# Delta rule over one chunk of all 32 heads at a time, in 64x64 tiles on the quadrants of the array

## The chip, the cores and the metric

One core of a Trainium2 chip runs the program. The metric is the device time of one execution in microseconds (us). Times of parts come from one execution that the hardware profiler took. The engines are named PE (TensorE, matmuls), PEld (TensorE's weight loads, which overlap PE), DVE (VectorE), ACT (ScalarE), POOL (GpSimd) and SP (SyncE, which issues most DMAs).

## What is computed

The first stage is a delta rule over 4 batches x 8 heads, 768 tokens, head size 48, all float32. The second sends each token to one of 8 experts by the largest logit, and an expert keeps at most 80 tokens, those with the largest gate weight.

```python
k_n = k / (np.linalg.norm(k, axis=-1, keepdims=True) + 1e-06)
state = np.zeros((B, H, D, D))
for t in range(S):
    y[:, :, t] = einsum('bhd,bhde->bhe', q[:, :, t], state)
    v_old = einsum('bhde,bhd->bhe', state, k_n[:, :, t])
    state = state + beta[:, :, t, None, None] * einsum('bhd,bhe->bhde', k_n[:, :, t], v[:, :, t] - v_old)
x = y.transpose(0, 2, 1, 3).reshape(B * S, H * D)          # 3072 x 384
# mixture of experts: 8 experts, hidden size 1024, capacity 80
logits = x @ w_gate; expert_idx = argmax(logits); gate_w = softmax(logits)[expert_idx]
for e in range(8):
    tok_idx = the at most 80 tokens of expert e with the largest gate_w
    out[tok_idx] = gate_w[tok_idx, None] * (np.maximum(x[tok_idx] @ w1[e], 0) @ w2[e])
```

## The kernel before

The delta rule runs in chunks of C = 64 tokens. Within a chunk, with A[t, s] = beta_s k_t.k_s for s < t, it is Z = (I + A)^-1 (V - K S), U = beta Z, y = Q S + (Q K^T, s < t) U, S += K^T U. The inverse is built from blocks of width 1, 2, 4 to 64: five levels after the first, each with a product P2 of B1 (which holds I + A transposed) and X, masked, then a new X and its transpose Y.

A tile holds two heads: 128 rows are (head of the pair, token of the chunk), and the matrices that multiply them are block-diagonal over the two heads, 128x128 with two zero blocks. A step is one chunk of one batch: four pairs of heads side by side, 128x512 in one PSUM bank. There are 48 steps, handled two at a time.

`prep(i)` (L229 to L289) makes what a step needs without the state: the scaled k and a copy of q go into block-diagonal tiles `kbd` and `qbd` on POOL (L234, L236), four transposes each give KT and QT (L241, copied by ACT at L242), K K^T and Q K^T are products (L246, L248) whose evictions on DVE apply beta and the mask (L251, L252), two selects and a product on POOL make B1 and the first Y (L253 to L258), and a transpose of B1 gives the first X (L262, L264). Each of the five levels has a product (L269) evicted by DVE with a mask (L271), a product (L276) copied by ACT to X (L278) and the transpose of X (L283) copied by ACT to Y (L287); the last level makes Y alone, by a product (L285).

`chain(i)` (L294 to L350) is the part that needs the state: K S (L303), R = V - K S on DVE (L305), Z and U (L309, L311), y (L317, L318) copied by ACT (L331) and written by two DMAs to `x_rows` in DRAM (L334), the new state (L322, L328; kept in SBUF, added on DVE), and the gate's logits by a transpose and small products (L338 to L349, 64 weight columns, 8 moving).

`weave` (L421) takes one stage of each of its generators in turn, so the order of every engine's queue is: one stage of the chains of two steps, one stage of each of the next two preps, and so on. In the loop at L439 each pass handles two steps of one batch. PSUM holds five one-bank buffers for prep (`ps_m`) and three for the chain (`ps_c`). `norms(b)` (L190) gives the inverse norms of k for a whole batch; `load(b)` (L153) loads k, q and v of a batch on the SP queue. `gate(b)` (L352) turns a batch's logits into weights and keeps the 80 best candidates by ten rounds of maxima and replacements (L408, L409) on DVE.

After the last step, the candidates are gathered by six DMAs into `mg` (L484), the threshold is found on DVE (L489, L491), slots are computed, and tokens are gathered and sent through the experts (L568 on). Expert matrices are 16 tiles of 1.57 MB loaded by `load_w` on the SP queue: WR0 = 4 of them during the delta rule, six (WR - WR0) when its memory is free (L460), the others as experts finish.

In the profile a float32 product is two matmul instructions with a weight load each; a transpose is one of each.

Of the kernel before, what the change touches and what calls it, by code (L numbers as in the profile page):

```python
# [24 lines left out]
def kernel(  # L25
# [26 lines left out]
    NP = H // 2  # L52
# [5 lines left out]
    NM = B * NT  # L58
# [4 lines left out]
    PD = NP * D  # L63
    GP = 2 * D
    assert NP == 4 and GP <= 128 and NT * E <= 128 and 2 * E * NM <= 512

# [9 lines left out]
    strict = const.tile([128, 128], F32, name="strict")  # L76
    nc.gpsimd.memset(strict, 1.0)
    nc.gpsimd.affine_select(out=strict, in_=strict, compare_op=Alu.is_gt, fill=0.0, base=0,
                            pattern=[[1, 128]], channel_multiplier=-1)
# [7 lines left out]
    for w in widths:  # L87
        m = const.tile([128, 128], F32, name=f"mask{w}")
        nb = 128 // (2 * w)
        mv = m.rearrange("p (g j) -> p g j", g=nb)  # L90
        nc.gpsimd.memset(mv[:, :, w:], 0.0)
        lo = mv[:, :, 0:w]
        nc.gpsimd.memset(lo, -1.0)
        nc.gpsimd.affine_select(out=lo, in_=lo, compare_op=Alu.is_ge, fill=0.0, base=-w,
                                pattern=[[-2 * w, nb], [0, w]], channel_multiplier=1)
        nc.gpsimd.affine_select(out=lo, in_=lo, compare_op=Alu.is_ge, fill=0.0, base=2 * w - 1,
                                pattern=[[2 * w, nb], [0, w]], channel_multiplier=-1)
        nc.gpsimd.affine_select(out=m, in_=m, compare_op=Alu.not_equal, fill=1.0, base=0,
                                pattern=[[1, 128]], channel_multiplier=-1)
        masks.append(m)  # L100
    mask1T = const.tile([128, 128], F32, name="mask1T")
    nc.gpsimd.memset(mask1T, 0.0)
    odd = mask1T.rearrange("p (g j) -> p g j", j=2)[:, :, 1:2]
    nc.gpsimd.memset(odd, -1.0)
    nc.gpsimd.affine_select(out=odd, in_=odd, compare_op=Alu.is_equal, fill=0.0, base=0,
                            pattern=[[-2, 64], [0, 1]], channel_multiplier=1)
    nc.gpsimd.affine_select(out=mask1T, in_=mask1T, compare_op=Alu.not_equal, fill=1.0, base=0,
                            pattern=[[1, 128]], channel_multiplier=-1)
# [5 lines left out]
    hii = const.tile([128, NM], I32, name="hii")  # L114
    nc.gpsimd.iota(hii, pattern=[[2, NM]], base=0, channel_multiplier=0)
    hi = const.tile([128, NM], F32, name="hi")
    nc.gpsimd.tensor_copy(hi, hii)
    pp1i = const.tile([128, 1], I32, name="pp1i")
    nc.gpsimd.iota(pp1i, pattern=[[1, 1]], base=1, channel_multiplier=1)
    pp1 = const.tile([128, 1], F32, name="pp1")  # L120
    nc.gpsimd.tensor_copy(pp1, pp1i)

    beta_t = keep.tile([128, B, NP, NC], F32, name="beta_t")
    wg = keep.tile([GP, NP // 2, 2, E], F32, name="wg")
# [6 lines left out]
    WR0, WR = 4, 10  # L131
# [10 lines left out]
    with ExitStack() as actx:  # L142
        inp = actx.enter_context(tc.tile_pool(name="inp", bufs=2))
        blk = actx.enter_context(tc.tile_pool(name="blk", bufs=1))
        mat = actx.enter_context(tc.tile_pool(name="mat", bufs=4))
        vec = actx.enter_context(tc.tile_pool(name="vec", bufs=3))
# [4 lines left out]
        kin, qin, vin, inv, state = {}, {}, {}, {}, {}  # L151

        def load(b):  # L153
            if b >= B:
                return
            for lst, nm, src in ((kin, "kin", k), (qin, "qin", q), (vin, "vin", v)):
                t = inp.tile([128, NP, NC, D], F32, name=nm)
                for h in range(H):
                    p, e = divmod(h, 2)
                    nc.sync.dma_start(t[64 * e : 64 * e + 64, p],  # L160
                                      src[b, h].rearrange("(c t) d -> t c d", t=C))
                lst[b] = t

        half = B // 2 * NP * NC
        bt = blk.tile([half, 2, 2, C], F32, name="bt")
        for j in range(2):
            for e in range(2):
                for r in range(half // NC):
                    b, p = divmod(r + j * (half // NC), NP)
                    nc.scalar.dma_start(bt[r * NC : (r + 1) * NC, j, e, :],  # L170
                                        beta[b, 2 * p + e].rearrange("(c t) -> c t", t=C))
        load(0)
        for h in range(H):
            p, e = divmod(h, 2)
            g, p2 = divmod(p, 2)
# [14 lines left out]
        def norms(b):  # L190
            if b >= B:
                return
# [426 lines left out]
```

## Time and profile before

| | |
|---|---|
| runs, median (lowest to highest) | 1162.03 us (1161.6 to 1165.42) |
| span of the profiled execution | 1162.0 us |
| instructions | 21302, of them 8825 matmuls and as many weight loads |
| PE busy | 1056.7 us |
| DVE, ACT, POOL busy | 439.1, 326.7, 236.3 us |

A span counts from the first to the last instruction of the program. Busy times of PE and PEld overlap, and matmuls are pipelined: the recorded duration of one (some 280 ns) is longer than the distance to the next, so a pace is read from a run of equal instructions in the timeline.

### The profile page before, as it was taken

To read this page: it belongs to the slowest core of one execution; us is meant where nothing else is said; L and a number is where in the kernel's file an instruction comes from. 1 tells how busy PE (TensorE), PEld (TensorE's weight loads), DVE (VectorE), ACT (ScalarE), POOL (GpSimd) and SP (SyncE) were. 2 spreads that over 40 slices of the span, in tenths; PEclk is the share of its full clock that TensorE was granted. 3 is DMA by queue.
4 is the path that set the end of the run, shared out by engine and by line. 5 is a ranking of instruction groups with operands and counts; after the bars stand their busy time and mean duration, and the time that the engine had idled before them with its cause. 6 is when DMAs were issued, how large, how long until landed. Compare 5 with 4: busy or idle time off the path is not lost. (4 is left out here: it accounts for less than half of the span.)

```text
span 1162.0 us, 21302 instructions
## 1 busy us (share of the span) xinstructions
PE 1056.7 (91%) x8825; PEld 993.7 (86%) x8825; DVE 439.1 (38%) x982; ACT 326.7 (28%) x609; POOL 236.3 (20%) x436
## 2 busy tenths in 40 slices
PE   0799999999999999999999999999999999704998
PEld 0789999999999999999999999998999999704775
DVE  3352333433433624534335333344345323364010
ACT  1234223423322343333234223333332342100000
POOL 3320222032212202221220223023112201002000
PEclk9999999999999999999999999999999999755999
DMA  7930401400200005002000000000000000361820
GB/s 119 211 140 18 155 7 23 71 8 11 43 5 7 6 5 89 5 5 48 8 5 5 8 5 7 6 8 5 5 8 8 5 5 8 93 241 34 275 72 13
DMA packets 116863, 52.22 MB, mean 45 GB/s; under 512 B 103456, under 2 KB 111648, under 8 KB 116768
## 3 DMA queue, kind: packets, MB, share of 16 engines
q1 hardware_dynamic: 114720, 48.79, 17.8%
q0 software_dynamic: 768, 1.97, 0.6%
q8 instruction: 70, 1.15, 0.4%
q10 hardware_dynamic: 1280, 0.11, 0.1%
q14 instruction: 25, 0.20, 0.1%
HBM read 40.42 MB, written 10.42 MB: 44 GB/s over the span
## 5 line engine op out<-in xcount | busy, mean ns | idle before, releaser
L269 PE MATMUL pm<-X,B 128*128 128x128 f32 x1920 | 244.1, 281 | 3.6 <-DVE X L264 3.4
L269 PEld LDWEIGHTS pm<-X,B 128*128 128x128 f32 x1920 | 228.2, 195 | 8.9 <-DVE X L264 8.4
L271 DVE TENSOR_TENSOR P<-pm,mask 128x512 f32<-128x512 f32 x240 | 165.5, 690 | 172.7 <-PE pm L269 168.7
L278 ACT COPY X<-pm 128x512 f32<-128x512 f32 x192 | 112.4, 585 | 363.5 <-PE pm L276 363.4
L276 PE MATMUL pm<-P,Y 128*128 128x128 f32 x1536 | 195.4, 280 | 1.0 <-DVE ohg L388 0.5
L276 PEld LDWEIGHTS pm<-P,Y 128*128 128x128 f32 x1536 | 179.5, 191 | 9.3 <-issue 2.6
L287 ACT COPY Y<-pm 128x512 f32<-128x512 f32 x240 | 138.4, 588 | 104.7 <-PE pm L285 63.3
L283 PE MATMUL pm<-ident,X 128*128 128x128 f32 x768 | 117.4, 281 | 5.2 <-ACT X L278 3.5
L236 POOL COPY qbd<-qin 64x192 f32<-64x192 f32 x96 | 32.7, 342 | 387.8 <-PE pm L241 382.9
L283 PEld LDWEIGHTS pm<-ident,X 128*128 128x128 f32 x768 | 85.0, 145 | 16.2 <-ACT X L278 14.8
L234 POOL TENSOR_TENSOR kbd<-kin,inv 64x192 f32<-64x192 f32 x96 | 48.9, 509 | 220.3 <-PE pc L322 199.4
L318 PE MATMUL pc<-U,PT 128*128 128x48 f32 x384 | 73.0, 277 | 0.3 <-DVE U L311 0.2
L331 ACT COPY xs<-pc 128x192 f32<-128x192 f32 x48 | 15.3, 318 | 188.6 <-PE pc L318 188.3
L317 PE MATMUL pc<-st,QT 128*128 128x48 f32 x352 | 66.2, 270 | 0.0
L258 POOL TENSOR_TENSOR Y<-B,mask1T 128x512 f32<-128x512 f32 x48 | 60.9, 1269 | 4.0
L311 DVE TENSOR_TENSOR U<-pc,beta_t 128x192 f32<-128x192 f32 x48 | 17.2, 358 | 111.2 <-PE pc L309 111.2
L318 PEld LDWEIGHTS pc<-U,PT 128*128 128x128 f32 x384 | 58.3, 195 | 0.5 <-DVE U L311 0.5
L317 PEld LDWEIGHTS pc<-st,QT 128*128 128x128 f32 x352 | 54.4, 195 | 0.0
L246 PE MATMUL pm<-KT 128*128 128x128 f32 x384 | 53.1, 282 | 0.0
L248 PE MATMUL pm<-QT,KT 128*128 128x128 f32 x384 | 51.6, 278 | 0.0
L579 PEld LDWEIGHTS hp<-xTe,w 128*128 128x128 f32 x384 | 49.0, 210 | 2.1 <-issue 1.2
L285 PE MATMUL pm<-Y,P 128*128 128x128 f32 x384 | 49.0, 280 | 0.5
(153 smaller groups left out, 1232.8 us busy)
## 6 DMA issues: line engine op xcount, KB each, us to landing
w<-in_moe_w_dram SPq DMA_DIRECT2D x16, 1536.0 KB
kin<-in_k_dram SPq DMA_DIRECT2D x32, 144.0 KB
qin<-in_q_dram SPq DMA_DIRECT2D x32, 144.0 KB
vin<-in_v_dram SPq DMA_DIRECT2D x32, 144.0 KB
x_rows<-xs SPq DMA_DIRECT2D x96, 48.0 KB
out_dram<-zero SPq DMA_DIRECT2D x12, 384.0 KB
bt<-in_beta_dram ACTq DMA_DIRECT2D x32, 3.0 KB
wg<-in_moe_w_gate_dram ACTq DMA_DIRECT2D x8, 1.5 KB
```

Source lines behind the costliest of these rows:

```text
L246: nc.tensor.matmul(pk[:, p, :], lhsT=KT[:, p, :], rhs=KT[:, p, :], start=True, stop=True)
L248: nc.tensor.matmul(pq[:, p, :], lhsT=KT[:, p, :], rhs=QT[:, p, :], start=True, stop=True)
L258: nc.gpsimd.tensor_tensor(out=Y, in0=B1, in1=over_pairs(mask1T), op=Alu.mult)
L269: nc.tensor.matmul(pp[:, p, :], lhsT=B1[:, p, :], rhs=X[:, p, :], start=True, stop=True)
L271: nc.vector.tensor_tensor(out=P2, in0=pp, in1=over_pairs(masks[n]), op=Alu.mult)
L276: nc.tensor.matmul(px[:, p, :], lhsT=Y[:, p, :], rhs=P2[:, p, :], start=True, stop=True)
L278: nc.scalar.copy(X, px)
L283: nc.tensor.transpose(py[:, p, :], X[:, p, :], ident)
L285: nc.tensor.matmul(py[:, p, :], lhsT=P2[:, p, :], rhs=Y[:, p, :], start=True, stop=True)
L287: nc.scalar.copy(Y, py)
L317: nc.tensor.matmul(py[:, p, :], lhsT=QT[:, p, :], rhs=state[b][:, p, :], start=True, stop=False)
L318: nc.tensor.matmul(py[:, p, :], lhsT=PT[:, p, :], rhs=U[:, p, :], start=(c == 0), stop=True)
```

## The change

The work is cut the other way: a block is one chunk of all 32 heads, and there are 12 blocks. Heads are named by (g, p, e): row half e (partitions 0 to 63 or 64 to 127), bank p, and one of NQ = 8 places g. A matrix of one head is 64x64 on one half of the partitions, with no zero blocks, and 32 of them fill a tile of 128 x 2 x 8 x 64 (two PSUM banks). Every product except the transposes of K, Q and x and the logits is done per head, with 64 (or 48) contracted rows and up to 64 output rows, so it uses one quadrant of the array: the row half of its operands and the column half of its output. `tiles` emits the 32 products so that consecutive ones go to the quadrants (0, 0), (1, 1), (0, 1), (1, 0) in turn, and the table `lv` says in which half and bank each level's results stand, so that tiles of different row halves write different banks.

- `prep(c)`: K and Q are transposed from unpadded pairs of heads (16 transposes per block, 128x128). B1 is turned into X by a product with `eye` instead of a transpose; Y is made at each level as a product of P2 and the old Y, not as a transpose of X. Evictions are two halves of 128 x 512 each. The copy of q on POOL is gone (q is loaded into `qn` directly); the selects on B1 are done per half of the partitions, over 1024 columns.
- `chain(c)`: Q S and the masked Q K^T U are evicted separately and added on DVE. The state is accumulated by PE in PSUM (`S_ps`, two banks) and copied to SBUF by ACT. x of a block is 128 rows (two batches) x 2 x 384.
- PSUM: `ps_m` has three buffers of two banks, used by prep, chain and gate alike; `S_ps` has the other two banks.
- Loads are per chunk (`load_k`, `load_q`, `load_v`), norms too. `w_gate` is loaded by one DMA. WR0 is 2 instead of 4.
- Loop: pass c weaves `chain(c)`, the second half of `prep(c + 1)` (7 stages) and the first half of `prep(c + 2)` (7 stages). The gate runs once every three blocks.

```diff
-    WR0, WR = 4, 10
+    WR0, WR = 2, 10
...
-        mat = actx.enter_context(tc.tile_pool(name="mat", bufs=4))
+        mat = actx.enter_context(tc.tile_pool(name="mat", bufs=3))
-        ps_m = actx.enter_context(tc.tile_pool(name="ps_m", bufs=5, space=PSUM))
-        ps_c = actx.enter_context(tc.tile_pool(name="ps_c", bufs=3, space=PSUM))
+        ps_m = actx.enter_context(tc.tile_pool(name="ps_m", bufs=3, space=PSUM))
+        ps_s = actx.enter_context(tc.tile_pool(name="ps_s", bufs=1, space=PSUM))
...
+        def mtile():
+            return ps_m.tile([128, 2, 512], F32, name="pm", tag="m")
...
+        def tiles(where, emit, byhead=False):
+
+            cls = {}
+            for e, p, g in HEADS:
+                cls.setdefault(where(e, p, g) if byhead else where(e, p), []).append((e, p, g))
+            order = [kk for kk in ((0, 0), (1, 1), (0, 1), (1, 0)) if kk in cls]
+            for n in range(max(len(x) for x in cls.values())):
+                for kk in order:
+                    if n < len(cls[kk]):
+                        emit(*cls[kk][n])
...
+        def halves(fn):
+            for n in range(2):
+                fn(slice(4 * n, 4 * n + 4))
...
+            KT = mat.tile([128, NQ, 128], F32, name="KT")
+            QT = mat.tile([128, NQ, 128], F32, name="QT")
+            for dst, src in ((KT, kb), (QT, qb)):
+                pt = mtile()
+                for g in range(NQ):
+                    nc.tensor.transpose(pt[:, g // 4, (g % 4) * 128 : (g % 4) * 128 + 128],
+                                        src[:, 2 * g : 2 * g + 2, :].rearrange("r p d -> r (p d)"), ident)
+                for n in range(2):
+                    nc.scalar.copy(dst[:, 4 * n : 4 * n + 4], pt[:, n].rearrange("r (g w) -> r g w", w=128))
+            yield
+            pk, pq = mtile(), mtile()
+            for ps, r in ((pk, KT), (pq, QT)):
+                tiles(lambda e, p: (p, e),
+                      lambda e, p, g: nc.tensor.matmul(ps[hs(e), p, 64 * g : 64 * g + 64],
+                                                       lhsT=KT[hs(p, D), g, hs(e)], rhs=r[hs(p, D), g, hs(e)],
+                                                       start=True, stop=True))
...
+            px = mtile()
+            tiles(lambda e, p: (e, e),
+                  lambda e, p, g: nc.tensor.matmul(px[hs(e), p, 64 * g : 64 * g + 64],
+                                                   lhsT=B1[hs(e), p, g], rhs=eye[hs(e)], start=True, stop=True))
+            X = mat.tile([128, 2, NQ, 64], F32, name="X", bufs=2)
...
+            lv = {1: (EE, PP, PP, PP, EE), 2: (PP, EE, PP, EP, PP), 3: (EP, EE, EP, PP, EP), 4: (PP, EE, PP, EP, PP),
+                  5: (EP, EE, None, EP, PP)}
+            xb, yb = PP, PP
+            for n in range(1, len(widths)):
+                f, pb, xo, yh, yo = lv[n]
+                last = n == len(widths) - 1
+                pp = mtile()
+                tiles(lambda e, p: (e, f(e, p)),
+                      lambda e, p, g: nc.tensor.matmul(pp[hs(f(e, p)), pb(e, p), 64 * g : 64 * g + 64],
+                                                       lhsT=B1[hs(e), p, g], rhs=X[hs(e), xb(e, p), g],
+                                                       start=True, stop=True))
+                P2 = mat.tile([128, 2, NQ, 64], F32, name="P2", bufs=2)
+                halves(lambda s: nc.vector.tensor_tensor(out=P2[:, :, s], in0=sq4(pp)[:, :, s], in1=wide(masks[n]), op=Alu.mult))
                 yield
+                if not last:
+                    px = mtile()
+                    tiles(lambda e, p: (f(e, p), e),
+                          lambda e, p, g: nc.tensor.matmul(px[hs(e), xo(e, p), 64 * g : 64 * g + 64],
+                                                           lhsT=Y[hs(f(e, p)), yb(e, p), g],
+                                                           rhs=P2[hs(f(e, p)), pb(e, p), g], start=True, stop=True))
+                    X = mat.tile([128, 2, NQ, 64], F32, name="X", bufs=2)
+                    halves(lambda s: nc.scalar.copy(X[:, :, s], sq4(px)[:, :, s]))
+                    xb = xo
+                py = mtile()
+                tiles(lambda e, p: (f(e, p), yh(e, p)),
+                      lambda e, p, g: nc.tensor.matmul(py[hs(yh(e, p)), yo(e, p), 64 * g : 64 * g + 64],
+                                                       lhsT=P2[hs(f(e, p)), pb(e, p), g],
+                                                       rhs=Y[hs(f(e, p)), yb(e, p), g], start=True, stop=True))
+                Y = mat.tile([128, 2, NQ, 64], F32, name="Y")
+                halves(lambda s: nc.scalar.copy(Y[:, :, s], sq4(py)[:, :, s]))
+                yb = yo
...
             if c < NC - 1:
+                tiles(lambda e, p: (e, p),
+                      lambda e, p, g: nc.tensor.matmul(S_ps[hs(p, D), e, g * D : g * D + D], lhsT=kb[hs(e), 2 * g + p, 0:D],
+                                                       rhs=U[hs(e), e ^ p, g], start=False, stop=False,
+                                                       skip_group_check=True))
+                st = vec.tile([128, 2, NQ, D], F32, name="st")
+                halves(lambda s: nc.scalar.copy(st[:, :, s], d48(S_ps)[:, :, s]))
+                St[0] = st
...
+        NSTG = 14
+        HALF = 7
         norms(0)
+        norms(1)
+        preps = {0: prep(0), 1: prep(1)}
+        weave(steps(preps[0], NSTG), steps(preps[1], HALF))
         for i in range(WR0):
             load_w(i)
         gates = iter(())
+        for c in range(NC):
+            load_k(c + 3)
+            load_q(c + 2)
+            load_v(c + 1)
+            norms(c + 2)
+            gens = [chain(c)]
+            if c + 1 < NC:
+                gens.append(preps.pop(c + 1))
+            if c + 2 < NC:
+                preps[c + 2] = prep(c + 2)
+                gens.append(steps(preps[c + 2], HALF))
             weave(*gens)
```

## Rows read from the trace of the kernel before

**Rows 1.** The page's shares: busy time, share of the span and instructions by engine.

```profile
PE 1056.7 (91%) x8825; PEld 993.7 (86%) x8825; DVE 439.1 (38%) x982; ACT 326.7 (28%) x609; POOL 236.3 (20%) x436
```

**Rows 2.** Busy time by stage, in windows: opening, steady stretch, last chain, selection, experts.

```profile
core 0: us, PE busy (x) PEld busy (x) DVE busy (x) ACT busy (x) POOL busy (x), PEclk, DMA share, GB/s
28.70:68.20 39.50, 32.81 (x239) 30.27 (x240) 12.99 (x20) 13.54 (x24) 11.65 (x22) 1.00 1.26 256
68.20:1001.00 932.80, 917.17 (x7972) 882.34 (x7970) 371.80 (x810) 301.92 (x563) 195.66 (x333) 0.99 0.09 19
1001.00:1013.30 12.30, 10.23 (x51) 9.14 (x50) 1.86 (x7) 0.32 (x1) 1.37 (x7) 0.50 0.44 142
1013.30:1060.00 46.70, 3.75 (x28) 2.40 (x28) 33.45 (x100) 0.00 (x0) 2.28 (x7) 0.50 0.47 169
1060.00:1162.00 102.00, 91.94 (x536) 69.18 (x536) 8.84 (x23) 7.00 (x16) 14.85 (x16) 0.90 0.34 112
```

**Rows 3.** Paces: timeline rows (start, us), then groups by shape (busy us, mean ns).

```profile
301.91 1.95 PE L269 MATMUL pm<-X,B 128*128 128x128 f32 x16
311.07 0.97 PEld L309 LDWEIGHTS pc<-vin,Y 128*128 128x128 f32 x8
322.17 0.54 PEld L347 LDWEIGHTS pc<-wg,xT 96*64 96x64 f32 x8 [0.17 <-issue]
1012.12 0.93 PEld L347 LDWEIGHTS pc<-wg,xT 96*64 96x64 f32 x8 [0.94 <-DVE xT L341]
...
L269 PE MATMUL pm<-X,B 128*128 128x128 f32 x1920 | 244.1, 281 | 3.6 <-DVE X L264 3.4
L309 PEld LDWEIGHTS pc<-vin,Y 128*128 128x128 f32 x32 | 3.9, 191 | 0.1
L347 PEld LDWEIGHTS pc<-wg,xT 96*64 96x64 f32 x384 | 26.7, 141 | 8.5 <-issue 3.5 <-DVE xT L341 1.9 <-DVE ss L198 0.3
```

**Rows 4.** Groups on the other engines by shape: busy us, mean ns of one.

```profile
L271 DVE TENSOR_TENSOR P<-pm,mask 128x512 f32<-128x512 f32 x240 | 165.5, 690 | 172.7 <-PE pm L269 168.7 <-issue 3.1
L278 ACT COPY X<-pm 128x512 f32<-128x512 f32 x192 | 112.4, 585 | 363.5 <-PE pm L276 363.4
L305 DVE TENSOR_TENSOR R<-vin,pc 128x192 f32<-128x192 f32 x44 | 15.6, 354 | 87.0 <-PE pc L303 86.8
L331 ACT COPY xs<-pc 128x192 f32<-128x192 f32 x48 | 15.3, 318 | 188.6 <-PE pc L318 188.3
L253 POOL TENSOR_SCALAR_AFFINE_SELECT B<-B 128x512 f32<-128x512 f32 x48 | 30.4, 634 | 69.6 <-DVE B L251 69.6
L258 POOL TENSOR_TENSOR Y<-B,mask1T 128x512 f32<-128x512 f32 x48 | 60.9, 1269 | 4.0
L234 POOL TENSOR_TENSOR kbd<-kin,inv 64x192 f32<-64x192 f32 x96 | 48.9, 509 | 220.3 <-PE pc L322 199.4 <-DVE inv L213 17.4
L198 DVE TENSOR_REDUCE ss<-sq 128x12 f32<-128x576 f32 x16 | 11.7, 744 | 6.5 <-ACT sq L197 6.4
L378 DVE SCALAR_TENSOR_TENSOR ex<-ex,r 128x48 f32<-128x48 f32 x24 | 5.0, 208 | 0.8
L408 DVE MAX8 cand<-cand 48x8 f32<-48x208 f32 x40 | 14.7, 368 | 1.2
```

**Rows 5.** Timeline of the opening: the ACT queue's DMA issues, and PE's first transposes.

```profile
0.79 14.43 ACTq L170 DMA_DIRECT2D bt<-in_beta_dram  x32
15.26 3.90 ACTq L176 DMA_DIRECT2D wg<-in_moe_w_gate_dram  x8
28.70 1.11 PE L241 MATMUL pm<-ident,kbd 128*128 128x128 f32 x4 [11.22 <-POOL kbd L234]
```

**Rows 6.** Timeline of the selection, and the weights' transfer in a window inside it.

```profile
1027.97 4.21 SPq L484 DMA_DIRECT2D mg<-cand  x6
1036.83 0.65 DVE L489 MAX8 top<-mg 8x8 f32<-8x480 f32 x1 [8.54 <-DMA mg<-cand]
1016.00:1032.00 16.00, 0.38 (x1) 0.12 (x1) 10.65 (x43) 0.00 (x0) 1.53 (x5) 0.50 1.05 395
```

More of the change, by code (lines that the diff above doesn't have):

```diff
@@ L100 @@
+        nc.gpsimd.tensor_tensor(out=m, in0=m, in1=eye, op=Alu.add)
         masks.append(m)
-    mask1T = const.tile([128, 128], F32, name="mask1T")
+    mask1T = const.tile([128, 64], F32, name="mask1T")
     nc.gpsimd.memset(mask1T, 0.0)
[L103 to L106, printed above, removed]
@@ L110 @@
+    nc.gpsimd.tensor_tensor(out=mask1T, in0=mask1T, in1=eye, op=Alu.add)
     revi = const.tile([128, E], I32, name="revi")
@@ new lines, in load_v @@
+        def load_v(c):
+            if c >= NC:
+                return
+            vin[c] = inp.tile([128, 2, NQ, D], F32, name="vin", bufs=3)
+            src = vf.rearrange("(q p e) (c t) d -> p e c t q d", p=2, e=2, t=C)
+            for p in range(2):
+                for e in range(2):
+                    h = e ^ p
+                    nc.sync.dma_start(vin[c][64 * h : 64 * h + 64, p], src[p, e, c])
+        HB = BH // 4
+        bt = blk.tile([HB * NC, 2, 2, C], F32, name="bt")
+        load_k(0)
@@ L166 @@
+        bsrc = bf.rearrange("(j g e) (c t) -> j e g c t", j=2, e=2, t=C)
         for j in range(2):
             for e in range(2):
[L168 to L175, printed above, removed]
-            nc.scalar.dma_start(wg[D * p2 : D * p2 + D, g, e, :], w_gate[h * D : h * D + D, :])
@@ new lines @@
+        for t in kn + qn:
+            nc.vector.memset(t[:, :, D:], 0.0)
+        load_q(0)
+        load_k(1)
+        load_v(0)
+        load_q(1)
+        load_k(2)
+        nc.scalar.dma_start(wg, w_gate.rearrange("(j p) n -> p j n", p=128))
+        def mtile():
+            return ps_m.tile([128, 2, 512], F32, name="pm", tag="m")
+        bps = mtile()
+        for j in range(2):
+            nc.tensor.transpose(bps[:, j, : HB * NC], bt[:, j].rearrange("r e t -> r (e t)"),
+                                ident[: HB * NC, : HB * NC])
@@ new lines, with norms @@
+        for j in range(2):
+            nc.vector.tensor_copy(beta_t[:, :, :, j * 4 : j * 4 + 4],
+                                  bps[:, j, : HB * NC].rearrange("r (q p c) -> r c p q", p=2, c=NC))
+        nc.vector.tensor_copy(beta_u[0:64], beta_t[0:64])
+        for p in range(2):
+            nc.vector.tensor_copy(beta_u[64:128, :, p, :], beta_t[64:128, :, 1 - p, :])
+        S_ps = ps_s.tile([128, 2, 512], F32, name="S_ps")
+        nc.vector.memset(S_ps, 0.0)
+        def norms(c):
+            if c >= NC:
+                return
+            sq = sml.tile([128, NB, D], F32, name="sq")
+            nc.scalar.activation(sq, kr[c], Act.Square)
+            ss = sml.tile([128, NB], F32, name="ss")
+            nc.vector.tensor_reduce(ss, sq, axis=AX, op=Alu.add)
+            seed = sml.tile([128, NB], U32, name="seed")
@@ new lines, in norms, with row, grp @@
+            iv = sml.tile([128, NB], F32, name="inv")
+            nc.vector.reciprocal(iv, n)
+            nc.gpsimd.tensor_tensor(out=kn[c % NKB][:, :, 0:D], in0=kr.pop(c),
+                                    in1=iv.unsqueeze(2).to_broadcast([128, NB, D]), op=Alu.mult)
+        HEADS = [(e, p, g) for e in range(2) for p in range(2) for g in range(NQ)]
+        def row(g):
+            return g // 2 % 2
+        def grp(g):
+            return g // 4 * 2 + g % 2
+        def tiles(where, emit, byhead=False):
[7 more added lines that the diff above has]
+                        emit(*cls[kk][n])
@@ L426, in weave, with steps @@
                         live.remove(g)
-        def chains(j):
-            yield from chain(2 * j)
-            yield from chain(2 * j + 1)
-        NS = len(steps) // 2
+        def steps(g, n):
+            for _ in range(n):
+                if next(g, g) is g:
+                    return
+                yield
+        NSTG = 14
+        HALF = 7
         norms(0)
-        load(1)
-        weave(prep(0), prep(1))
+        norms(1)
+        preps = {0: prep(0), 1: prep(1)}
+        weave(steps(preps[0], NSTG), steps(preps[1], HALF))
         for i in range(WR0):
```

363 lines of the change are left out of this document (164 added, 199 removed).

## The prediction

> **What bounds the kernel now.** I read the page's shares first: TensorE (PE) is busy 91% of the span, VectorE 38%, ScalarE 28%, GpSimd 20% [rows 1]. The windows by stage say where [rows 2]: PE starts at 28.7 us, the delta rule holds it until 1013.3 us (984.6 us), then 46.7 us are selection on VectorE with almost no PE, then 102 us are the experts. In the steady stretch PE is busy 917 of 932.8 us.
>
> What bounds PE is read from the pace of its instructions. A float32 product is two passes, each a weight load and a matmul (I call this a pair); a transpose is one. In the timeline sixteen pairs of L269 (128 weight columns, 128 moving) take 1.95 us: less the 281 ns of the last one, 15 paces of 111 ns. Eight pairs of L309, same weights but only 48 moving columns, take as long each: (0.97-0.191)/7 = 111 ns for the loads. Eight pairs of L347, 64 weight columns and 8 moving, come (0.54-0.141)/7 = 57 to 58 ns apart [rows 3]. So a pair costs its weight load, about 1.2 columns per ns plus 5 ns; moving fewer columns buys nothing. 7970 pairs in 932.8 us are 117 ns each, where the pure mix (mostly 111, one in twenty at 58) would be 109: 7% is lost.
>
> **The change, part by part.** *Pairs.* Per chunk of 32 heads and per product 32 tiles of 64x64, two passes: 64 pairs. Prep has 17 products (K K, Q K, the turn of B1 against `eye`, 5 P2, 4 X, 5 Y): 1088 pairs; the chain has 5 (two less work: the first chunk lacks two, the last lacks one): 320. In all 12 x 1408 - 192 = 16704 pairs with 64 weight columns or fewer, and 34 wide instructions per chunk (16+6 transposes, 12 gate pairs), 408. Before, the same stretch had some 8260. The products with zeros are gone, but PE gets twice the instructions, each with half the load time: if loads stay one after another, 16704 x 58 = 969 us, plus 408 x 0.11 = 45 us, is 1014 us against some 900 us of pure pace now (8260 x 109 ns). That is the crux: **the change gains only what quadrants overlap.** No instruction of the trace shares the array with another tile, so it is unknown. Bounds from the nearest row, L347: 58 ns (nothing overlaps) and 14.5 ns (four quadrants, each at 58). I take 29 ns, two at a time: loads of tiles on rows 0-63 and on rows 64-127 read different partitions, and `tiles` alternates those halves at each step, so I expect them side by side; two tiles on the same 64 partitions I expect to queue for each other, as every two loads in the trace do (L269: 1.2 columns per ns however dense the stream). Both are assumptions. Then 16704 x 29 = 484 us, plus 45 us: 529 us, or 44.6 us per full chunk (1408 x 29 ns + 34 x 110 ns).
>
> *What must hide under that.* The other engines have room now: before the eviction at L278 alone ScalarE waits 363 us for PE. VectorE per chunk: 16 half evictions of 512 columns at 0.69 = 11.0; R and U 4 x 0.56 and x and xT 2 x 0.96 (from 0.69 at 512 and 0.354 at 192 columns, 1.05 ns a column) = 4.1; norms one reduce (744 ns x 768/576 = 0.99) and 13 small ones at 0.2 (L378) = 3.6; logits 0.2; a third of a gate, some 20 small ones and ten rounds of 0.37 for the maxima and as much for their removal, = 4. Sum 23 us. ScalarE: 22 copies of 512 at 0.59 = 13.0, x 0.80, st 2 x 0.48, squares 0.92: 15.7 us. GpSimd: four selects over 1024 columns at 1.27 (twice the 0.635), Y 2.5, the scaled k 4 x 0.51: 9.7 us [rows 4]. All are under 44.6 us, so PE stays the bound, and the halved eviction work earns nothing by itself.
>
> *Cover of the waits.* PSUM goes from eight one-bank buffers to three of two banks (the state has the other two), 25 fills per chunk. [...] The slack is thinner than before, so I put the steady loss at 10% instead of 7%. B1 is late next: two selects in place per half of the partitions (5.1 us on GpSimd) stand between K K and the turn of B1; PE has the other prep and the chain in between, some 6 us a round (84 rounds in all). Without that cover it costs up to 12 x 5 us. The waits PE does have, in its queue, are held in order: a late chain step stops both preps behind it.
>
> *Changes of tile shape.* Wide and 64x64 work alternates some six times per chunk, 72 times. Not in the trace; bounds 0 and the 281 ns that a matmul is in flight: I take its excess over the pace, 281-111 = 0.17 us, 12 us in all.
>
> *Start.* The 32 beta issues (14.43 us on ScalarE's queue) stay; one w_gate issue replaces eight (3.9 us); the norms of one chunk need one reduce and not four. First PE work about 25 us instead of 28.7 [rows 5]. The opening, one and a half preps in 14 rounds (27 fills, 50 us), has little to weave; I add 8 us.
>
> *Tail.* Two expert matrices instead of four are loaded early, so two more (2 x 1.573 MB at the 395 GB/s shown = 8 us) stand in the SP queue's transfers ahead of the six `mg` copies, for whose landing VectorE already waits 8.5 us [rows 6]. Bounds 0 (the longer last chain hides it) and 8 us: 4 us.
>
> *Sum at 29 ns.* Opening 50 + 8; ten per cent on the middle, (529 - 50 - 11) x 1.10 = 515; the last chunk's chain alone 11 + 8; shape changes 12: 604 us. 25 + 604 + (1162.0 - 1013.3 = 148.7) + 4 = **782 us**. Span and the runs' median (1162.03) agree, so nothing is added.
>
> [...] By the columns and starts above, nothing paces PE but loads: L347 starts an instruction every 29 ns, which is just half its 58 ns load. [...]
>
> **The rivals.** *Serial, slower.* PE does one load at a time whichever tile it is for. For it: every pair in the trace, 48 or 128 columns, runs at the pace of its load, and loads come one after another. Against it: the two row halves share no partition. Then 1014 us pure: opening 100 + 5, middle (1014-100-22) x 1.05 = 937, end 30, shapes 12: 1084; 25 + 1084 + 148.7 + 4 = 1262 us. Between this and 782 us a nanosecond per pair is worth 16.6 us, so it decides from 52 ns up: there the kernel is slower than now.
>
> *Issue-bound.* The sequencer, not the array, sets some 22 ns per instruction, between the 14.5 that my forecast needs and the 29 that L347 shows: 44.5 ns a pair, 743 + 45 = 788 us pure. Opening 84, middle 743, end 25, shapes 12: 864; 1042 us (36 to 51 ns: 900 to 1150).
>
> *Four at a time.* 14.5 ns: fills of 0.93 us, 242 + 45 us pure, 24 us a chunk. VectorE at 23 us and the three buffers, (0.93 + 0.3 + 1.38)/3 = 0.87 us each for 25 fills = 22 us, are then as long, and in-order waits between 7 rounds add some 5: 30 us a chunk. 42 + 11 x 30 + 16 = 388; 25 + 388 + 152.7 = 566 us, to 730 us if the waits are worse.
>
> **How the numbers follow.** Forecast (25 to 36 ns, 710 to 900 us) 0.38; issue-bound 0.20; four at a time 0.23; serial 0.19. The likeliest gives 782 us. The range leaves out the serial case alone: from 565 to 1110 us. Faster by over 0.3% (about what a measurement of this kernel can tell): the first three but for a sliver, 0.79; within it 0.02; slower 0.19.
>
> **What would show it.** In the profile after: pace of the 64x64 pairs in the timeline, 29 ns (58: serial; 44: issue; 15: four); some 17,650 PE pairs with the experts' 536; VectorE near 23 us a chunk and PE's idle time small. If VectorE or the buffers are named ahead of long PE gaps, the four-way case or a failed cover is at work. Wide transposes should keep 109 to 111 ns. `mg` landing later would show the tail's term; a first PE instruction past 29 us would refute the start's. [...]

## The result, and the profile after

The changed kernel takes 738.64 us (735.01 to 747.89), against 1162.95 us for the kernel before on the same chip: a ratio of 0.6337 [0.6319, 0.6355]. 782 us was forecast, 5.9% too much, with a range from 565 to 1110 us. The longest of the four runs here (747.89 us), and the 755.23 us of the kernel with `mg` on ScalarE's queue further down, are slow runs, which the ratios leave out (mean granted clock 0.879 and 0.715, against 0.883 to 0.899 in the other runs of the two kernels). The profiled execution has a span of 733.3 us; the sums below are made against that.

From the page of the kernel after (busy time, share, instructions; then PE's busy tenths and granted clock in 40 slices; then the queue that brings instructions to the engines, with packets, MB and share):

```profile
span 733.3 us, 37473 instructions
PE 505.5 (69%) x17681; PEld 456.2 (62%) x17681; DVE 297.4 (41%) x745; ACT 174.5 (24%) x326; POOL 140.8 (19%) x198
PE   0567578767786685968878677786857200499997
PEclk9969989999899999998789999899999655589999
q8 instruction: 139, 2.28, 1.3%
```

PE has twice the pairs of before [rows 1] and half the busy time, and nothing is near full: PE fell from 91% to 69%, VectorE rose only from 38% to 41%. So by the shares no engine binds the kernel as a whole. The last line is easily passed over; before, the same queue had 70 packets in 1162 us:

```profile
q8 instruction: 70, 1.15, 0.4%
```

The windows by stage of the kernel after (start and end; busy us and instructions of each engine; granted clock, DMA share, GB/s) answer to [rows 2]:

```profile
25.50:95.90 70.40, 48.67 (x1696) 46.12 (x1696) 38.05 (x100) 20.76 (x38) 18.35 (x13) 0.85 0.55 130
95.90:556.00 460.10, 345.83 (x14947) 324.64 (x14951) 201.15 (x477) 139.95 (x263) 87.88 (x79) 0.94 0.16 35
556.00:574.60 18.60, 13.99 (x486) 13.06 (x478) 5.42 (x9) 3.93 (x7) 1.39 (x7) 0.89 0.21 64
574.60:636.00 61.40, 4.61 (x34) 3.15 (x33) 34.28 (x106) 0.00 (x0) 5.27 (x10) 0.50 0.54 200
636.00:733.30 97.30, 91.63 (x535) 68.83 (x533) 8.18 (x16) 7.01 (x16) 11.91 (x13) 0.92 0.35 116
```

The steady stretch has 14947 pairs in 460.1 us: 30.8 ns each, almost the 29 ns of the forecast. It is the same number for another reason, as the timeline shows (weight loads of PE in the kernel after: start, us; the last column is idle time and what ended it):

```profile
304.14 1.02 PEld L353 LDWEIGHTS pm<-X,B 64*64 64x64 f32 x64
305.07 1.95 PEld L362 LDWEIGHTS pm<-P,Y 64*64 64x64 f32 x64
...
310.96 0.79 PEld L353 LDWEIGHTS pm<-X,B 64*64 64x64 f32 x47 [0.86 <-issue]
312.75 1.09 PEld L362 LDWEIGHTS pm<-P,Y 64*64 64x64 f32 x64 [1.00 <-issue]
313.75 0.33 PEld L370 LDWEIGHTS pm<-Y,P 64*64 64x64 f32 x16
314.88 0.79 PEld L370 LDWEIGHTS pm<-Y,P 64*64 64x64 f32 x48 [0.80 <-issue]
315.58 1.03 PEld L393 LDWEIGHTS pm<-st,KT 48*64 48x64 f32 x64
316.51 0.33 PEld L398 LDWEIGHTS pm<-st,QT 48*64 48x64 f32 x16
318.79 0.79 PEld L398 LDWEIGHTS pm<-st,QT 48*64 48x64 f32 x48 [1.95 <-issue]
```

*The array's pace.* The 64 loads of L353 at 304.14 take 1.02 us; less the 0.135 us of the last one that is (1.02-0.135)/63 = 14.0 ns a pair. All four quadrants work at once. L362 at 305.07 is the first level, whose tiles lie on the two diagonal quadrants only (so do those of the turn of B1, of the first P2 and of the last Y, four of the 22 products): (1.95-0.135)/63 = 28.8 ns. So one quadrant takes 58 ns a pair, as L347 did before [rows 3], and quadrants don't hold each other up.

*The stops.* Four rows are idle before they start, with "issue" as what ended it: PE's loads waited for nothing that the profile shows. At 312.75 us PE's matmuls wait for VectorE's P2. The other three stops fall inside a product, after 17 or 16 of its 64 pairs, where no semaphore stands between two tiles. From 310.96 to 314.88 us are 47 + 64 + 16 = 127 pairs, from 314.88 to 318.79 are 48 + 64 + 16 = 128: PE stops after every 254 to 256 instructions, 3.92 and 3.91 us apart. The first interval holds the wait of 1.00 us at 312.75, the second none, and yet both are as long. At 14.0 ns, 128 pairs are 1.8 us of array.

*What comes in blocks.* In the trace's records of queue q8, a packet (2.28 MB / 139 = 16 KB) begins 2.2 to 2.9 us before each stop ends, and the next begins 1.0 to 3.5 us after that (median 1.2). PE's loads and matmuls, 35362, over 139 packets are 254 per packet. Between 25 us and the end of the delta rule there are 86 places where over 0.5 us pass between two starts of PE's instructions with no semaphore to wait for; PE is idle 106.5 us in them, and 83 of them lie inside one product. Counted with the instructions of PE's sequencer, which the lists above leave out, all 86 begin at the same place of a block of 256. The steady stretch is 14947 x 2 / 255 = 117 blocks, 3.9 us each. Before, a packet held as many (17650/70 = 252), but the array needed 14.7 us for one (7970 pairs in 932.8 us), and no such stop is in the trace.

So the reading is: **PE's instructions are delivered in blocks of some 255, a block comes every 3.9 us here, and that, not the array, paces the delta rule**: 3.9/255 = 15.3 ns an instruction, 30.6 ns a pair. Why a block is not brought earlier, the runs do not show.

### The profile page after: what moved, and what is told of

It reads as the page before. It is cut to its first block, busy times and chain, and to the rows that moved or that the text cites. A ratio compares the mean times of both kernels' runs of the same rounds, so it can differ in the third digit from the quotient of the medians.

```text
span 733.3 us, 37473 instructions
## 1 busy us (share of the span) xinstructions
PE 505.5 (69%) x17681; PEld 456.2 (62%) x17681; DVE 297.4 (41%) x745; ACT 174.5 (24%) x326; POOL 140.8 (19%) x198
## 3 DMA queue, kind: packets, MB, share of 16 engines
q8 instruction: 139, 2.28, 1.3%
## 5 line engine op out<-in xcount | busy, mean ns | idle before, releaser
L357 DVE TENSOR_TENSOR P<-pm,mask 128x512 f32<-128x512 f32 x120 | 77.1, 684 | 111.8 <-PE pm L353 111.7
L353 PE MATMUL pm<-X,B 64*64 64x64 f32 x3840 | 93.9, 230 | 28.4 <-issue 28.4
L366 ACT COPY X<-pm 128x512 f32<-128x512 f32 x96 | 51.5, 589 | 232.3 <-PE pm L362 232.3
L353 PEld LDWEIGHTS pm<-X,B 64*64 64x64 f32 x3840 | 83.8, 143 | 32.5 <-issue 32.3
L370 PE MATMUL pm<-Y,P 64*64 64x64 f32 x3840 | 87.4, 223 | 20.1 <-issue 18.3
L370 PEld LDWEIGHTS pm<-Y,P 64*64 64x64 f32 x3840 | 79.7, 138 | 23.0 <-issue 22.9
L362 PE MATMUL pm<-P,Y 64*64 64x64 f32 x3072 | 76.6, 228 | 23.6 <-DVE P L357 11.2
L362 PEld LDWEIGHTS pm<-P,Y 64*64 64x64 f32 x3072 | 69.5, 141 | 29.0 <-issue 22.9
L330 POOL TENSOR_SCALAR_AFFINE_SELECT B<-B 64x1024 f32<-64x1024 f32 x24 | 27.5, 1147 | 287.1 <-DVE B L324 276.9
L374 ACT COPY Y<-pm 128x512 f32<-128x512 f32 x120 | 64.7, 595 | 38.9 <-PE pm L370 38.9
L340 PEld LDWEIGHTS pm<-eye,B 64*64 64x64 f32 x768 | 30.8, 163 | 11.2 <-POOL B L332 8.5
L332 POOL TENSOR_SCALAR_AFFINE_SELECT B<-B 64x1024 f32<-64x1024 f32 x24 | 27.5, 1147 | 1.6
```

Of the source, the lines that this page charges most:

```text
L330: nc.gpsimd.affine_select(out=bv[hs(e)], in_=bv[hs(e)], compare_op=Alu.is_gt, fill=0.0, base=0, pattern=[[0, 2 * NQ], [1, 64]], channel_mu ...
L332: nc.gpsimd.affine_select(out=bv[hs(e)], in_=bv[hs(e)], compare_op=Alu.not_equal, fill=1.0, base=0, pattern=[[0, 2 * NQ], [1, 64]], channe ...
L340: lambda e, p, g: nc.tensor.matmul(px[hs(e), p, 64 * g : 64 * g + 64], lhsT=B1[hs(e), p, g], rhs=eye[hs(e)], start=True, stop=True))
L353: lambda e, p, g: nc.tensor.matmul(pp[hs(f(e, p)), pb(e, p), 64 * g : 64 * g + 64], lhsT=B1[hs(e), p, g], rhs=X[hs(e), xb(e, p), g], start ...
L357: halves(lambda s: nc.vector.tensor_tensor(out=P2[:, :, s], in0=sq4(pp)[:, :, s], in1=wide(masks[n]), op=Alu.mult))
L362: lambda e, p, g: nc.tensor.matmul(px[hs(e), xo(e, p), 64 * g : 64 * g + 64], lhsT=Y[hs(f(e, p)), yb(e, p), g], rhs=P2[hs(f(e, p)), pb(e, ...
```

## The experiments

The theory is delivery in blocks. Its rivals are the forecast's array (two tiles at a time, 29 ns), a four-way array whose evictions and buffers bound (the third rival of the prediction), and, for the first kernels, queueing on the same partitions.

**Fewer quadrants at a time.** The loop in `tiles` is replaced. One quadrant after another:

```diff
-            for n in range(max(len(x) for x in cls.values())):
-                for kk in order:
-                    if n < len(cls[kk]):
-                        emit(*cls[kk][n])
+            for kk in order:
+                for x in cls[kk]:
+                    emit(*x)
```

> The 32 tiles of a product are issued quadrant by quadrant (8 on one, then 8 on the next), nothing else changes. If quadrants overlap only when neighbours in the stream lie on different ones, the pace falls back to 58 ns a pair and PE sets the time: about 1014 us of pure pace, some 1200 to 1260 us in all. If the gain over the kernel before came from something else (half the eviction work, fewer waits), the time stays near 739 us.

Two quadrants at a time, on different row halves, or (third kernel) on the same rows, the pairs being `((0, 0), (0, 1))` and `((1, 0), (1, 1))`:

```diff
+            for both2 in (((0, 0), (1, 1)), ((0, 1), (1, 0))):
+                for n in range(8 if len(order) == 4 else 16):
+                    for kk in both2:
+                        if kk in cls and n < len(cls[kk]):
+                            emit(*cls[kk][n])
```

> Two quadrants alternate that lie on different row halves, first (0,0) and (1,1), then (0,1) and (1,0); never four. Instruction delivery theory (PE's instructions arrive in blocks of 256 at no less than some 3.6 us each, 14 ns an instruction, 28 ns a pair; the array itself does four at a time at 14.5 ns): the pace in the timeline falls to 29 ns a pair, but that is what delivery gives anyway, so 740 to 790 us. My forecast (the array does two at a time already): the same pace as now and 739 us. Array theory (four at a time is what made the kernel fast): pure pace doubles by 242 us, some 900 us or more.

> Two quadrants alternate that share a row half and differ in the column half, first (0,0) and (0,1), then (1,0) and (1,1). My forecast assumed that two tiles on the same 64 partitions queue for each other: then 58 ns a pair and some 1200 us, as with one quadrant at a time. If they overlap like tiles on different rows: 29 ns a pair, and the time of the run with two row halves, 740 to 800 us (three of the 22 products use only two quadrants, which this order runs one after the other: up to 40 us more).

Measured: one quadrant 1477.38 us and two on the same rows 1024.0 us (single runs, no interval); two row halves 746.79 us (743.22 to 748.43), ratio 0.6411 [0.6387, 0.6435]. The steady stretch in windows (columns as above): of the one-quadrant kernel, of two row halves, and of two on the same rows; then a run of loads in the timeline of two row halves, and a line of its page:

```profile
100.00:1300.00 1200.00, 1187.02 (x16045) 1175.12 (x16044) 219.76 (x531) 156.23 (x288) 87.58 (x79) 0.63 0.06 14
```

```profile
100.00:560.00 460.00, 421.38 (x14653) 406.57 (x14649) 195.56 (x472) 138.37 (x257) 87.72 (x79) 1.00 0.15 33
```

```profile
100.00:900.00 800.00, 735.89 (x15952) 719.98 (x15948) 235.85 (x585) 153.10 (x282) 91.28 (x93) 0.66 0.14 37
```

```profile
318.33 1.78 PEld L354 LDWEIGHTS pm<-X,B 64*64 64x64 f32 x64
```

```profile
PE 600.2 (80%) x17681; PEld 556.7 (75%) x17681; DVE 295.7 (40%) x745; ACT 176.4 (24%) x326; POOL 140.5 (19%) x198
```

With two row halves the array's pace is (1.78-0.14)/63 = 26 ns, nearly half the speed of the kernel after, and PE's busy time over the span rises by 95 us, from 505.5 to 600.2; the time rises by 8 us. The array has that much to spare: in the steady stretches shown, PE's idle time shrinks from 114 us of 460.1 to 39 us of 460, and the stops without a semaphore from 86 to 48. The work fills the stops. That settles that the array is not the bound.

One quadrant is slower than expected, and two on the same rows lie between the two values expected; the windows say why: the granted clock is 0.63 and 0.66 there. Most loads of one quadrant start 58 ns apart at a granted clock of 1.00 and 107 ns at 0.50; over a whole product it is less (64 pairs of one, from 449.46 to 452.48 us at full clock, are 47 ns each), because at the switch from one quadrant to the next their work overlaps. So nothing overlaps inside one quadrant, as expected. Two tiles on the same rows do overlap, though: loads start in twos, 58 ns from two to two at full clock. The assumption that tiles on the same 64 partitions queue for each other **fell**; that kernel is slow mostly by its clock: 570 of its 903 us of PE's busy time are at the lower level (0.50), and with that part at twice the pace 618 us would be left (an estimate), against the 600 us of two row halves. The products that use two diagonal quadrants only, four and not three as expected, run one quadrant after the other there; what they cost was not tried by itself.

**More instructions, hardly more array work.** An extra tile with one moving column goes ahead of a quarter of the tiles of each product but the state's; the tile behind it overwrites what it wrote. In the first kernel it has one weight column too, in the second 40, so that it is a 64x64 tile like the others:

```diff
+        def mm(out, lhsT, rhs, start, stop):
+            if small[0]:
+                w = min(40, lhsT.shape[-1])
+                out, lhsT, rhs = out[0:w, 0:1], lhsT[:, 0:w], rhs[:, 0:1]
+            nc.tensor.matmul(out, lhsT=lhsT, rhs=rhs, start=start, stop=stop)
```

> Ahead of a quarter of the tiles of every product but the state's, a tile of one weight column and one moving column is issued into a place that the full tile then overwrites: some 32 more PE instructions per product, 24% more in all, with next to no work for the array and none for the other engines. Instruction delivery theory: 139 blocks of 256 become some 171, at 3.6 to 3.8 us each 115 to 120 us more: 850 to 860 us. Forecast (29 ns a pair on the array) and the theory that evictions and PSUM buffers set the time: at most the start spacing of 16 small pairs per product, 740 to 770 us.

> As the run with small extra tiles, but the extra tiles have 40 weight columns (and one moving column), so they are on the same 64x64 quadrants and the shape of the array doesn't change. Instruction delivery theory: 24% more PE instructions, 139 blocks become some 171, 115 to 120 us more: 850 to 860 us. Forecast (two quadrants at a time): 16 extra pairs a product at (40/1.2+5)/2 = 19 ns, 21 products, 12 blocks: 77 us more, 815 us. Four quadrants on the array with time set by evictions: 740 to 760 us. The loss of the small extra tiles (920 us) is laid to changes of tile shape; if it was the number of instructions, this run loses as much.

The first took 1659.41 us (1656.73 to 1661.04), ratio 1.4263 [1.4237, 1.429]: no theory had that. Its loads in the timeline, one row for each product:

```profile
410.98 5.35 PEld L313 LDWEIGHTS pm<-P,Y 64*1 64x1 f32 x80 [1.03 <-issue]
416.44 5.32 PEld L313 LDWEIGHTS pm<-Y,P 64*1 64x1 f32 x80
```

They are 5.46 us apart for 80 pairs, and none of it is idle. A load of one column is another tile shape, and each change of shape holds PE up, as the term "changes of tile shape" said, here 16 times a product. That it is the change, and not the small tile, is in the trace: a one-column load starts 345 ns behind a full one at the clock's lower level and a full one 113 ns behind a one-column load, but two one-column loads start 3 ns apart (medians). The second kernel has the same number of instructions without the changes and took 856.53 us (855.22 to 861.02), ratio 0.7361 [0.7346, 0.7376]: the difference, 803 us, over 4000 changes (250 products, 16 each) is 0.20 us each, mostly at the lower level. Delivery expected 850 to 860 us for the second; the two-way array 815, evictions 740 to 760. Its page:

```profile
PE 614.9 (72%) x21681; PEld 560.6 (65%) x21681; DVE 297.9 (35%) x745; ACT 177.0 (21%) x326; POOL 140.6 (16%) x198
q8 instruction: 170, 2.79, 1.3%
```

43362 loads and matmuls over 170 packets are 255 each; 31 packets more cost 117.9 us, 3.80 us a packet, while PE stays idle 28% of the span. 4000 pairs at 14 ns would have been 56 us, if the array had had no time to spare.

**Fewer instructions, more array work.** At levels 1 to 4, Y becomes eight wide 128x128 transposes of X again, in place of 64 pairs; the work on VectorE and ScalarE stays the same. For it `prep` has 18 stages instead of 14, and the last level's product for Y goes to all four quadrants:

```diff
-                tiles(lambda e, p: (f(e, p), yh(e, p)),
-                      lambda e, p, g: nc.tensor.matmul(py[hs(yh(e, p)), yo(e, p), 64 * g : 64 * g + 64],
...
+                    for g in range(NQ):
+                        nc.tensor.transpose(py[:, g // 4, (g % 4) * 128 : (g % 4) * 128 + 128],
+                                            X[:, g].rearrange("r b w -> r (b w)"), ident)
...
```

> At levels 1 to 4 the new Y is made by eight wide transposes of X (as in the kernel before, one stage later than X, so prep has 18 stages and a half is 9) instead of 64 pairs: 448 of some 2880 PE instructions of a block go, 15.5%; eight transposes at 0.11 us take the array as long as 64 pairs at 14.5 ns. Evictions keep their number and size. Instruction delivery theory: 139 blocks become 118, at 3.6 to 3.8 us 75 to 80 us less: 655 to 675 us. Forecast (29 ns a pair on the array): 12 x (4 x 64 x 29 ns - 32 x 110 ns) = 47 us less, 690 us. If four quadrants at 14.5 ns were what sets the time: nothing gained, 739 us or more for the longer chain of stages.

668.73 us (666.18 to 674.99), ratio 0.5768 [0.5729, 0.5806], where delivery had expected 655 to 675, the two-way array 690 and the four-way array 739. A step of array work (eight transposes at 111 ns, 0.9 us) as long as the one removed (64 pairs at 14 ns, 0.9 us) saves 70 us of 739. Its page:

```profile
PE 482.3 (73%) x14993; PEld 428.3 (64%) x14993; DVE 295.4 (44%) x745; ACT 174.3 (26%) x326; POOL 140.6 (21%) x198
q8 instruction: 118, 1.93, 1.2%
```

29986/118 = 254 again, and 21 packets less give 69.9 us, 3.33 us each. More and fewer instructions both move the time by 3.3 to 3.8 us a block; that is what shows the theory. (What the new stages and the four quadrants of the last product bring by themselves was not tried.)

**The evictions.** P2's masked eviction, VectorE's largest group, is done twice:

```diff
-                halves(lambda s: nc.vector.tensor_tensor(out=P2[:, :, s], ...
+                for _ in range(2):
+                    halves(lambda s: nc.vector.tensor_tensor(out=P2[:, :, s], ...
```

> VectorE does each masked eviction of P2 twice (L357, the same values written again): 10 more instructions of 0.68 us per block, 6.9 us of VectorE, and each of five of the 25 PSUM buffers of a block held 1.4 us longer. Instruction delivery theory: PE waits for its instructions anyway, 739 to 760 us. Theory that evictions and buffers set the time: up to 12 x 6.9 = 83 us more, 800 to 820 us.

759.0 us (757.71 to 763.11), ratio 0.6534 [0.6508, 0.656]. 120 evictions of 0.68 us more, by which VectorE's busy time rises by 69 us (297.4 to 366.3), cost 20 us; evictions as the bound had expected 800 to 820 us. They are not the bound, but not far: PE's matmuls of the next product, L363 here, wait 36.8 us for P2 (total, times, longest) instead of 11.2:

```profile
PE pm L363 <- DVE P L358: 36.8, 22, 3.4
```

**The tail.** The six `mg` copies are issued on ScalarE's queue (`nc.scalar.dma_start` at L588) and not behind the expert matrices on SP's.

> The six small copies into mg are issued on ScalarE's queue instead of SP's, where eight expert matrices stand ahead of them (VectorE waits 17.4 us for them now, 8.5 us before the change). If they wait because they stand behind those transfers in one queue, the wait falls to some 3 to 6 us and the time by 10 to 14 us: 725 to 729 us. If the shared DMA engines are what they wait for, nothing changes: 739 us.

725.62 us (718.39 to 755.23), ratio 0.6239 [0.6198, 0.6279]: 13 us less, or 16 us between the medians of the three shorter runs of each. Timeline of the kernel after, then of this one (the copies on their queue, and the first maximum, which waits for them):

```profile
592.47 9.06 SPq L588 DMA_DIRECT2D mg<-cand  x6
607.57 0.65 DVE L593 MAX8 top<-mg 8x8 f32<-8x480 f32 x1 [17.39 <-DMA mg<-cand]
```

```profile
585.00 4.11 ACTq L588 DMA_DIRECT2D mg<-cand  x6
590.25 0.65 DVE L593 MAX8 top<-mg 8x8 f32<-8x480 f32 x1 [4.90 <-DMA mg<-cand]
```

VectorE's wait fell from 17.39 to 4.90 us, and that is the gain; some 5 us of it are the issuing itself (9.06 against 4.11 us).

**Towards a better kernel.** Three more follow the theory. `e11` is the kernel with transposed Y, and `mg` on ScalarE's queue. `e9` adds that K K^T and Q K^T become one product (K and Q in one tile `KQ`, one load for 128 moving columns), which leaves out 768 pairs:

```diff
...
+                      lhsT=KQ[hs(p, D), g, 0, hs(e)], rhs=KQ[hs(p, D), g, :, hs(e)], start=True, stop=True))
...
```

> The transposed Y and the mg copies on ScalarE's queue, without the joint product of K K and Q K: the reference for the two runs that have it. 668.7 less the 13 us of the tail: 656 us. If it comes at 652 us or less, the joint product brought nothing at all.

> The transposed Y and the mg copies on ScalarE's queue together, and K K and Q K as one product: one weight load of K serves 128 moving columns (K and Q side by side), so 64 of a block's remaining pairs go, with the same moving work for the array. About 20 blocks of 256 instructions fewer than with the transposed Y alone would be too many: 12 x 128 instructions are 6. Instruction delivery theory: 118 blocks become 112, at 3.3 to 3.8 us each 20 to 23 us less, and 13 us less in the tail: 632 to 638 us. Array theory (four quadrants at 14.5 ns): the same array time, so 656 us, from the tail alone.

`e11` took 664.92 us (662.01 to 668.11), ratio 0.5725 [0.5697, 0.5754]; `e9` 652.04 us (645.9 to 654.23), ratio 0.5598 [0.5561, 0.5636]. Both gain less than expected: the six blocks that `e9` saves against `e11` bring 13 us, 2.1 us each. In `e9` a wait has come up (page, then PE's largest wait for another engine in the delta rule, with total, times and longest):

```profile
PE 480.3 (74%) x14225; PEld 425.1 (66%) x14225; DVE 296.2 (46%) x745; ACT 174.2 (27%) x326; POOL 140.6 (22%) x198
q8 instruction: 112, 1.84, 1.1%
```

```profile
PE pm L343 <- POOL B L335: 25.5, 22, 3.3
```

28450/112 = 254 once more. But the turn of B1 now waits 25.5 us for GpSimd's selects; it waited 5.7 us in the kernel after and 8.8 us in `e11`. `e10` is `e9` with one more stage (a `yield`) between selects and turn, so that more work of others stands in between:

> The kernel with fewer instructions, with one more stage in prep between the selects on B1 and the product that turns it (19 stages, halves of 10 and 9), so that PE has a round of other work in between. In the run before it PE waited 25.5 us, 22 times, for those selects on GpSimd, against 5.7 us at first. If that wait ate the blocks that were saved, it goes and the time falls by 15 to 25 us from 652: 627 to 637 us. If PE then only waits for instructions or evictions elsewhere: 645 to 655 us.

649.64 us (647.63 to 652.58), ratio 0.5583 [0.557, 0.5595]: the second branch of what was expected, no gain that can be told. Waits of PE and of the first maximum in `e10`:

```profile
PE pm L344 <- POOL B L335: 9.3, 6, 3.5
PE pm L369 <- DVE P L364: 16.6, 18, 2.0
DVE top L608 <- DMA mg<-cand: 8.8, 1, 8.8
```

The wait for the selects fell from 25.5 to 9.3 us and another took its place: PE now stands before VectorE's evictions of P2. Of the stops without a semaphore 29 are left, with 30 us of PE's idle time (86 and 106.5 us in the kernel after), and packets begin 4.2 us apart on average. So delivery no longer sets the pace alone; PE is 75% busy, the engines are close to each other, and none yields much alone. It is the fastest kernel of all, though not told from `e9`, and 12% below the changed one. In `e11`, moving `mg` brought 4 us where it had brought 13: the wait is 8.8 us there, as in `e10`, against 4.90 us, and it was 15.7 us in the kernel with transposed Y. Expert matrices are in transfer meanwhile (DMA share 0.78 in `e11`, 0.65 with 4.90 us); why it lands sooner in one case was not tested and stays open.

## Why the prediction was right and where it was wrong

By its own steps, against the span of 733.3 us:

- *Count.* 16704 + 408 pairs and 569 others: 17681, as the page has it. Right.
- *Start.* The first transpose of K stands at 25.5 us; 25 was forecast. Right.
- *The pace, the crux.* 29 ns a pair was forecast, 30.8 measured; the **step that failed is the reason, "I expect two tiles on the same 64 partitions to queue for each other"**. They don't (two on the same rows overlap, and four quadrants run at 14.0 ns), so that the array alone was the rival of four at a time. What put the 30.8 ns back is a resource that the prediction didn't have: delivery of instructions, 15 ns each. Two errors of a factor of two met: that 29 ns came so near is luck, not the mechanism. The rival called issue-bound had the kind right (a price per instruction and not per column) and the size wrong, 22 ns, taken between two bounds; and a sequencer that takes that long for each would not show 64 pairs at 14.0 ns between two stops.
- *Starts and loads.* The trace has 64 matmuls of L353 in 1.16 us (at 304.14 us), some 15 ns apart, each with a load. So the tiles of four quadrants are in work at the same time, at four times the pace of one: 14.0 ns a pair against 58.
- *Middle.* 515 us and 12 us for changes of shape were forecast, 460.1 measured, 67 us less. The forecast added 10% for lost time, wide instructions at 110 ns and the changes of shape to the pace; the stretch measured is its 117 blocks of 3.9 us, with all of these in it. How much of them falls into PE's stops, as the wait of 1.00 us at 312.75 us did, was not tried; in the trace of the steady stretch a block of 256 instructions takes 4.4 us on average where it holds wide ones too (33 blocks) and 3.7 us where it holds none (84). The price of a change was about right: in the trace, at full clock, a quadrant tile starts 212 or 308 ns behind a wide one and a wide one 202 ns behind a quadrant tile, 0.09 to 0.20 us over the 111 ns between wide ones, where 0.17 was forecast. What of it lies on the path was not tried.
- *Cover of the waits.* Held in the steady stretch. PE's waits for VectorE's P2 and for GpSimd's selects, of the waits of the kernel after (total, times, longest), are small, and a half eviction takes the 684 ns in the page that it took before (690 [rows 4]); a select over 1024 columns takes 1147 ns, not 1270. No run shows the 0.3 us that stands beside fill and eviction in the third rival's sum, (0.93 + 0.3 + 1.38)/3: the handovers from PE to VectorE and back take 0.04 and 0.05 us in the trace before, 0.05 and 0.15 us in the one after (medians). The lines:

```profile
PE pm L362 <- DVE P L357: 11.2, 13, 0.9
PE pm L340 <- POOL B L332: 5.7, 4, 3.9
```

```profile
L357 DVE TENSOR_TENSOR P<-pm,mask 128x512 f32<-128x512 f32 x120 | 77.1, 684 | 111.8 <-PE pm L353 111.7
L330 POOL TENSOR_SCALAR_AFFINE_SELECT B<-B 64x1024 f32<-64x1024 f32 x24 | 27.5, 1147 | 287.1 <-DVE B L324 276.9
```

  VectorE still waits for PE, and not PE for it: 111.7 us before P2 alone. From VectorE's 244.6 us in the stretches up to 574.6, a block has 20.4 us (23 forecast), from ScalarE's 164.6 us 13.7 (15.7). For B1 that cover shrinks when the stream gets shorter (`e9`), as the forecast priced.
- *Opening.* 58 us forecast, 70.4 measured: 12 us more, the largest miss to this side. 1696 pairs are 13 blocks, 52 us at 3.9, and the granted clock was 0.85. PE is idle 21.7 us there: by the trace's stops over 0.5 us, 11.6 us where a block begins, 7.1 us for GpSimd's selects on B1 and 2.6 us for VectorE's P2. So part of it is the wait for B1 that the prediction priced but took to be covered.
- *Last chain.* 18.6 us, 19 forecast. Right.
- *Tail.* 158.7 us from the last logits on, 148.7 + 4 forecast. Of the 10 us more, 8.9 are VectorE's wait for `mg` (17.39 against 8.54 us [rows 6]). The mechanism was right, as `e7` shows; its size was the upper bound of 8 us and a little more, and the value between the bounds was the wrong one to take: the last chain did not hide it.

Sum of the differences: 0.5 + 12.4 - 66.9 - 0.4 + 6.0 = -48.4 us, which is 733.3 against 781.7.

The view that would have hinted at the delivery ahead of time was there: the page of before lists the packets of the instruction queue, and 252 instructions of PE to a packet. It had no price, since before a block lasted 14.7 us, but a block of the new stream would last 1.8 us on a four-way array, and the question what the queue can bring in that time would have been a rival with a chance of its own.

## What to carry to other kernels

Where a change replaces few large instructions by many small ones, count the instructions as well as the array's time: here 255 of them cost PE 3.3 to 3.9 us even where the array could do them in 1.8, so past that rate wide transposes (21 blocks and 70 us less here) or one load for two products (6 blocks and 13 us less) are worth more than a shorter tile. PE's idle time with nothing to wait for (86 places here, 83 of them inside a product), at equal distances (3.92 and 3.91 us above), is how this looks in a trace. Small copies that the end waits for do not belong in a queue behind bulk loads: their own queue brought 13 us here, and 4 us in the kernel with transposed Y.

## What the runs showed of the hardware that was not expected

- *Granted clock.* By the pages PE was busy 93% of the span with one quadrant at a time and 88% with two on the same rows, and the mean clock was 0.65 and 0.68; with two on different row halves, 80% busy, it was 0.94, and 1.00 in the steady stretch. Windows of the kernel with two on the same rows (loads of PE, granted clock):

```profile
410.00:420.00 10.00, 9.55 (x168) 0.51 0.22 41
420.00:430.00 10.00, 8.79 (x383) 1.00 0.24 44
450.00:460.00 10.00, 10.00 (x142) 0.50 0.01 2
```

The granted clock rose from 0.50 to 1.00 behind the wide transposes of K and Q (L312, here from 415.7 us on), so behind all ten such groups from 137 us on, and fell again in the small tiles. With one quadrant at a time it rose behind seven of the ten. What makes the difference was not tried and stays open.

- *Changes of tile shape.* Single columns among 64x64 tiles made the kernel 2.2 times as long (1659.41 against 738.64 us), 803 of the 921 us over the kernel with as many instructions and no changes, 0.20 us each. It ran at a mean clock of 0.571, but its trace has stretches at either level: a one-column load starts 345 ns behind a full one at the lower level and 200 ns at full clock, a full one 113 ns behind a one-column load at both.
- *Quadrants.* In float32 a pair costs 58 ns on one quadrant, and two or four quadrants overlap fully, 28.8 and 14.0 ns a pair.
